# S and dP of a cached attention decode step with K and V as the moving operand, packed into four column tiles of TensorE

## The chip, the cores and the metric

The kernel runs on one NeuronCore of a Trainium2 chip. Its time is the device time of one execution in microseconds (us); three runs before the change gave 403.45, 403.95 and 405.34, so the median is 403.95. Times inside an execution come from one profiled execution. TensorE multiplies matrices into PSUM, VectorE and ScalarE work on SBUF and PSUM, GpSimd and SyncE (SP) mostly issue DMAs here.

## The reference

One decode step of a gated mix of attention over a cache and an MLP, forward and backward. All inputs and outputs are bf16.

```python
def _A_ref(x, k_cache, v_cache, wq, wo):        # H = 32 heads, Sk = 4096, Dh = 128, D = 640
    q = (x @ wq).reshape(B, Sq, H, Dh)...
    scores = einsum("bhqd,bhkd->bhqk", q, k_cache) * (Dh ** -0.5)
    p = softmax(scores)
    o = einsum("bhqk,bhkd->bhqd", p, v_cache)
    return o.reshape(B, Sq, H * Dh) @ wo
def _B_ref(x, w1, b1, w2):                      # F = 1728, Mish
    h = x @ w1 + b1
    return (h * tanh(softplus(h))) @ w2
g = sigmoid((x * gate_w).sum(-1, keepdims=True))
out = g * _A_ref(...) + (1 - g) * _B_ref(...)
# outputs: out and the gradients of x, k_cache, v_cache, wq, wo, w1, b1, w2, gate_w for grad_out
```

With one query row, attention's backward pass needs, per head, dP = dO . V^T (one number per cached position), dS = P * (dP - D) with D = sum(dO * O), dV = P^T dO, dK = dS^T q, and dq = dS K. dK and dV are as large as the caches: 32 x 4096 x 128 each, so the kernel reads 82 MB and writes 82 MB.

## The kernel before, in words

The 32 heads are worked in 16 blocks of two heads (`i`, 0 to 15). In a block's K or V buffer (128 partitions x 8192 bf16, 2 MB) 64 partitions belong to each head and hold 64 positions each. There are seven such buffers; dV and dK are written over V and K and stored from there, and the freed buffer takes the next load. SP issues all loads in a fixed order (`loads`, `pump`); GpSimd issues most stores (`store_kv`).

A block is 16 slots (`slot(i, s)`), written out in order on every engine's queue. The weights `wq` and `wo` (four groups of eight heads) and the MLP are spread over the slots by tables (`plan`, `at`): the sums `do_sum` and `dx_sum` on VectorE, the products `dwo_row`, `dwq_row`, `mlp_dw2` on ScalarE or VectorE.

The scores need K transposed, dP needs V transposed. `transposes(b, c)` takes one eighth of a buffer: four float32 transposes on TensorE (a float32 is a pair of bf16, so a pair of d's stays together) into one of three PSUM tiles `tr`, and one ScalarE copy of 128x512 into a `tch` tile, of which there are NT = 4. In slots 0 to 7 these are V's eighths, in slots 8 to 15 those of the next block's K. `lagged` holds two of them back; then `products` makes eight matmuls from one `tch` tile (four parts t, two bf16 halves e), in which the transposed K or V is the stationary operand and a few columns of q or dO (`qR`, `dR`) move, 48 columns wide. They land in PSUM as `S` or `dP` with positions on the partitions, as the softmax wants them.

The chain of a block, in slots: `soft_max` (2, VectorE, from `S`), `soft_maxt` (4: transpose on TensorE, then negM on VectorE), `soft_exp` (5, ScalarE), `soft_z` (7), `soft_p` (8, ScalarE), `row_sum` for o (7 and 8, TensorE: 16 matmuls in four column tiles with V moving), `take` of o (8: ScalarE copies the PSUM tile into a `tch` tile), `o_post` (9: four transposes and four short VectorE steps), `d_sum` (10: a float32 matmul, then nD on VectorE), `ds_make` (11), the dV quarters `outer` (9, 10, 12, 13, VectorE), dq by `row_sum` (13, 14) and `take`, and the dK quarters (15 and, in the next block, 0, 1, 3). The last block (15) is written out after the loop, with the stores of dV and dK in halves, and then the small outputs from `frow`. Before the loop a prologue makes q, the first S and the first dO.

Of the kernel before, what the change touches and what calls it, by code (L numbers as in the profile page):

```python
# [17 lines left out]
def kernel(  # L18
# [49 lines left out]
    NT = 4  # L68
# [121 lines left out]
    ones_f = C([P, P], F32, "ones_f")  # L190
# [4 lines left out]
    qR = [C([P, 4, 2, 2, 2], BF16, f"qR{t}") for t in range(2)]  # L195
    dR = [C([P, 4, 2, 2, 2], BF16, f"dR{t}") for t in range(2)]
    for t in e_m + rs + ds_m:
        nc.vector.memset(t[:], 0.0)
    for t in qR + dR:
        nc.vector.memset(t[:].rearrange("p a b c d -> p (a b c d)"), 0.0)  # L200
# [12 lines left out]
    sel = C([P, 4, 16, 8], BF16, "sel")  # L213
    idv = idf[:].rearrange("p (a h d) -> p a h d", a=4, h=2)
    nc.vector.tensor_tensor(sel[:], idv[:, :, 0, :].unsqueeze(3).to_broadcast([P, 4, 16, 8]),
                            idv[:, :, 1, :].unsqueeze(3).to_broadcast([P, 4, 16, 8]), ALU.add)
# [46 lines left out]
    def pair_cols(dst):  # L263
# [6 lines left out]
        for jj in range(2):  # L270
            h = slice(64 * jj, 64 * jj + 64)
            nc.scalar.mul(dst[h, :, :, jj, :], tb[h], scale)
# [20 lines left out]
    def do_hot(g):  # L293
        nc.vector.tensor_tensor(R, sel[:], do8[g % 2][:].unsqueeze(1).unsqueeze(1).to_broadcast([P, 4, 16, 8]),
                                ALU.mult)
# [28 lines left out]
    def o_rows(g):  # L324
        ps = misc([P, 16, 8], F32, "o8_ps")
        nc.tensor.matmul(ps[:].rearrange("p a b -> p (a b)"), lhsT=od16[:].rearrange("p a b -> p (a b)"), rhs=idb[:],
                         start=True, stop=True)
        o8m = two.tile([P, 16, 8], F32, name="o8m", tag="o8m", bufs=1)
        nc.vector.tensor_tensor(o8m[:], ps[:], m16[:].unsqueeze(2).to_broadcast([P, 16, 8]), ALU.mult)
        nc.vector.reduce_sum(o8f[:], o8m[:].rearrange("p a b -> p b a"), axis=AX.X)  # L330
        nc.vector.tensor_copy(o8[:], o8f[:])
# [38 lines left out]
    def transposes(b, c):  # L370
        tp = tr_ps.tile([P, 4, P], F32, name="tr", tag="tr")
        src = fview(b)
        for t in range(4):
            nc.tensor.transpose(tp[:, t, :], src[:, 4 * c + t, :], idf[:])  # L374
# [5 lines left out]
    def products(ps, src, c, col):  # L380
        for t in range(4):
            B = 4 * c + t
            for e in range(2):
                nc.tensor.matmul(ps[:, 4 * B:4 * B + W].rearrange("p (a b) -> p a b", b=4),  # L384
                                 lhsT=src[:, t, :, e],
                                 rhs=col[:, e, :, :].rearrange("p a b -> p (a b)").unsqueeze(1).to_broadcast([P, W // 4, 4]),
                                 start=(e == 0), stop=(e == 1))

    S_ps, dP_ps, st = {}, {}, {}
# [5 lines left out]
    def soft_max(i):  # L395
        m = two.tile([P, 1], F32, name="m32", tag="m32")
        for hh in range(2):
            nc.vector.reduce_max(m[HS[hh]], sview(S_ps[i], hh), axis=AX.X)
        st[i] = dict(m=m)
# [9 lines left out]
    def soft_exp(i):  # L409
        for hh in range(2):  # L410
            nc.scalar.activation(e_m[i % 2][HS[hh], 0:J, hh], sview(S_ps[i], hh), ACT.Exp, bias=st[i]["negM"][HS[hh]],  # L411
                                 scale=1.0, accum_out=rs[i % 2][HS[hh], hh:hh + 1])

    def soft_z(i):
        z = chain([P, 2], F32, "z2")
        nc.tensor.matmul(z[:], lhsT=ones_f[:], rhs=rs[i % 2][:], start=True, stop=True)
# [27 lines left out]

    def own_cols(i, key, out):
# [14 lines left out]
    def d_sum(i):  # L460
        d = chain([P, 2], F32, "d2")
        nc.tensor.matmul(d[:], lhsT=ones_f[:], rhs=st[i]["od"][:], start=True, stop=True)
# [4 lines left out]
    def ds_make(i):  # L467
        ds = two.tile([P, J, 2], BF16, name="ds_dup", tag="ds_dup")
        for hh in range(2):
            nc.vector.scalar_tensor_tensor(ds_m[i % 2][HS[hh], 0:J, hh], in0=sview(dP_ps[i], hh),  # L470
# [265 lines left out]
    def lagged(i, s):  # L736
        pend.append((i, s))
        if len(pend) > 2:
            run_products(*pend.popleft())
# [3 lines left out]
    def run_products(i, s):  # L743
        src = work.pop((i, s))
        if s < 8:
            if s == 0:
                dP_ps[i] = one_ps.tile([P, 2 * J + W], F32, name="dP", tag="dP")
            products(dP_ps[i], src, s, dR[(i // 4) % 2][:, i % 4])
        else:
            n = i + 1  # L750
            if s == 8:
                S_ps[n] = one_ps.tile([P, 2 * J + W], F32, name="S", tag="S")
            products(S_ps[n], src, s - 8, qR[(n // 4) % 2][:, n % 4])
# [10 lines left out]
    def slot(i, s):  # L764
# [12 lines left out]
        elif pend:  # L777
            run_products(*pend.popleft())
        if i < 0:
            return  # L780
        if chain_on:
# [6 lines left out]
            if s == 2:  # L788
                soft_max(i)
            if s == 4:  # L790
                soft_maxt(i)
            if s == 7:
                soft_z(i)
        if s == 7:
            row_sum(i, "o", vbuf[i], e_m[i % 2], 0, 8)
        if s == 8:
            row_sum(i, "o", vbuf[i], e_m[i % 2], 8, 16)
            take(i, "o")
        if s == 10:
            d_sum(i)  # L800
# [6 lines left out]
        if s == 9:  # L807
# [24 lines left out]
    nc.tensor.matmul(z_ps[:], lhsT=ones_f[:], rhs=zp[:], start=True, stop=True)  # L832
# [32 lines left out]
    for c in range(8):  # L865
        run_products(-1, 8 + c)
        if c < 4:
            work[(-1, 12 + c)] = transposes(kbuf[0], 4 + c)
    for k in range(8):
# [41 lines left out]
    row_sum(i, "o", vbuf[i], e_m[i % 2], 8, 16)  # L911
    take(i, "o")
    last_dv(0)
    while pend:
        run_products(*pend.popleft())
    o_post(i)
    d_sum(i)
# [38 lines left out]
    nc.tensor.matmul(dg_ps[:], lhsT=ones_f[:], rhs=dgp[:], start=True, stop=True)  # L956
# [11 lines left out]
    frow = C([3, P, RC], BF16, "frow")  # L968
    nc.vector.tensor_copy(frow[:].rearrange("r p c -> r c p"), fr_ps[:])
    flat = frow[:].rearrange("r p c -> r (p c)")  # L970
# [36 lines left out]
```

## Time and profile before

| | |
|---|---|
| median of 3 runs | 403.95 us |
| profiled execution, its own time | 404.45 us |
| span of its instructions | 402.3 us |
| TensorE matmul busy | 303.7 us (76%), 4242 instructions |
| TensorE weight loads busy | 249.0 us (62%), 4249 instructions |
| VectorE busy | 293.4 us (73%) |
| ScalarE busy | 264.2 us (66%) |
| DMA | 164.71 MB, mean 409 GB/s |
| mean granted TensorE clock | 0.915 |
| `products` (L384) on TensorE | 2048 matmuls of 128x48, 94.8 us; their weight loads 89.7 us |
| `transposes` (L374) on TensorE | 1024 of 128x128 float32, 171.6 us |
| copies to `tch` (L377) on ScalarE | 256 of 128x512 at 0.587 us, 145.1 us |
| `take` (L443) on ScalarE | 128x512, 0.585 to 0.592 us each |
| dV and dK quarters (L480) on VectorE | 128 at 1.22 us, 153.6 us |

Busy times are of one execution; TensorE's overlap its weight loads, and the ends of its matmuls are modelled. The page cuts the span into 40 slices of about 10 us and gives the busy share of each in tenths; "DMA" there is the mean of the core's 16 DMA engines. "PEclk" is the clock that the throttle granted TensorE.

### The profile page before, as it was taken

What the parts mean: (1) busy time and instruction counts of PE and PEld (TensorE: products, weight loads), DVE (VectorE), ACT (ScalarE), POOL (GpSimd) and SP (SyncE); (2) the same over time, 40 slices, a digit from 0 to 9 for tenths busy, and PEclk for the clock granted to TensorE, in tenths of its full rate; (3) what the DMA queues carried; (4) which work ended last, traced back from release to release, by engine and by line L of the source; (5) the groups of instructions that cost most, each with busy time, mean ns of one, the idle gap of its engine ahead of it and who ended that gap; (6) DMA issues with size and microseconds to landing.
All of it is one profiled execution on the core that took longest, in us unless ns stands there. A gap on an engine that the chain in (4) does not pass through costs nothing.

```text
span 402.3 us, 10310 instructions
## 1 busy us (share of the span) xinstructions
PE 303.7 (76%) x4242; PEld 249.0 (62%) x4249; DVE 293.4 (73%) x650; ACT 264.2 (66%) x539; POOL 23.6 (6%) x47
## 2 busy tenths in 40 slices
PE   3879977987778675978889969845789898887410
PEld 3567866866567564866678748725568676675200
DVE  3759677789876595979887948751895697788770
ACT  3547453677567867787766668843377998876730
POOL 3000100001000010100001000000000000000000
PEclk9989998999899699999999989988699899999655
DMA  8999999999999999999999999999999999999992
GB/s 274 428 408 428 427 422 423 428 418 389 414 425 426 420 368 427 422 427 429 433 428 423 430 423 435 423 427 427 428 424 433 424 418 425 421 426 428 402 413 83
DMA packets 15867, 164.71 MB, mean 409 GB/s; under 512 B 1624, under 2 KB 1819, under 8 KB 6092
## 3 DMA queue, kind: packets, MB, share of 16 engines
q1 hardware_dynamic: 8842, 94.08, 55.8%
q0 software_dynamic: 5376, 63.42, 37.5%
q10 hardware_dynamic: 1602, 6.56, 4.3%
q8 instruction: 33, 0.54, 0.5%
q14 instruction: 14, 0.11, 0.1%
HBM read 82.03 MB, written 82.03 MB: 408 GB/s over the span
## 4 chain that ended last, share of the span: by engine, by line
DMA 31%; issue 20%; PE 18%; DVE 17%; ACT 9%; POOL 1%; SPq 1%; ACTq 0%; POOLq 0%; DVEq 0%
DMA wq<-in_A_wq_dram 10%; DVE kv L480 9%; PE tr L374 7%; DMA out_dram<-kv 6%; DMA wo<-in_A_wo_dram 6%; DMA wq<-in_B_w_dram 6%; DMA kv<-in_A_k_cache_dram 4%; ACT tch L377 3%; PE tr L448 2%; PE S L384 2%; DVE junk L290 1%; ACT p_dup L424 1%; PE dq L434 1%; PE a_ps L340 1%; ACT tch L443 1%
## 5 line engine op out<-in xcount | busy, mean ns | idle before, releaser
L377 ACT COPY tch<-tr 128x512 f32<-128x512 f32 x256 | 145.1, 587 | 65.3 <-PE tr L374 60.1
L374 PE MATMUL tr<-idf,kv 128*128 128x128 f32 x1024 | 171.6, 294 | 21.1 <-DMA kv<-in_A_v_cache_dram 10.5
L374 PEld LDWEIGHTS tr<-idf,kv 128*128 128x128 f32 x1024 | 119.7, 150 | 49.3 <-issue 32.4
L384 PEld LDWEIGHTS <-tch 128*128 128x128 bf16 x2048 | 89.7, 98 | 21.6 <-ACT tch L377 15.4
L480 DVE TENSOR_TENSOR kv<-p_dup,Dr 128x2048 bf16<-128x2048 bf16 x64 | 76.8, 1220 | 19.7 <-ACT p_dup L424 19.4
L480 DVE TENSOR_TENSOR kv<-ds_dup,Qr 128x2048 bf16<-128x2048 bf16 x64 | 76.8, 1220 | 0.4
L384 PE MATMUL dP<-dR,tch 128*128 128x48 bf16 x1024 | 47.1, 185 | 10.5 <-ACT tch L377 10.3
L384 PE MATMUL S<-qR,tch 128*128 128x48 bf16 x1024 | 47.7, 186 | 1.1 <-ACT tch L377 0.5
L290 DVE SCALAR_TENSOR_TENSOR junk<-wo,da_bc 128x640 bf16<-128x640 bf16 x32 | 26.3, 822 | 13.8 <-DMA wo<-in_A_wo_dram 13.1
L448 PE MATMUL tr<-idf,tch 128*128 128x128 f32 x128 | 22.0, 297 | 18.2 <-ACT tch L443 18.0
L757 POOL DMA_DIRECT2D out_dram<-kv x25 | 13.4, 536 | 297.1 <-DVE kv L480 251.9
L448 PEld LDWEIGHTS tr<-idf,tch 128*128 128x128 f32 x128 | 14.0, 145 | 20.8 <-ACT tch L443 19.8
L352 ACT ACTIVATE wq<-dqrow,xf 128x1024 bf16<-128x1024 bf16 (+2 forms) x30 | 25.1, 860 | 2.6 <-DVE wq L507 2.3
L507 DVE SCALAR_TENSOR_TENSOR wq<-wq,dqrow 128x1024 bf16<-128x1024 bf16 (+2 forms) x30 | 25.1, 863 | 0.2
L434 PE MATMUL o<-kv,e_m 128*32 128x512 bf16 x256 | 20.4, 400 | 0.0
L434 PE MATMUL dq<-kv,ds_m 128*32 128x512 bf16 x256 | 19.5, 384 | 0.9 <-DVE ds_m L470 0.9
L424 ACT ACTIVATE p_dup<-e_m,rz 64x128 bf16<-64x128 bf16 x32 | 12.7, 397 | 7.7 <-DVE rz L418 7.3
L352 ACT ACTIVATE wo<-da_bc,o8f 128x640 bf16<-128x640 bf16 x20 | 15.9, 825 | 1.3 <-PE a_ps L340 0.8
L411 ACT ACTIVATE e_m<-S,negM 64x64 bf16<-64x64 f32 x32 | 10.5, 329 | 6.3 <-DVE negM L406 5.7
L281 ACT CAST Qr<-q_ps 64x256 bf16<-64x256 f32 x16 | 5.9, 367 | 12.3 <-PE q_ps L277 12.2
L474 ACT COPY ds_dup<-ds_m 64x128 bf16<-64x128 bf16 x32 | 9.5, 296 | 6.4 <-DVE ds_m L470 5.8
L602 DVE SCALAR_TENSOR_TENSOR junk<-wq,db_bc 128x640 bf16<-128x640 bf16 (+1 forms) x14 | 11.5, 820 | 1.9 <-ACT db_bc L256 1.7
(169 smaller groups left out, 279.2 us busy)
## 6 DMA issues: line engine op xcount, KB each, us to landing
out_dram<-kv POOLq DMA_DIRECT2D x25, 2048.0 KB, 16.7
kv<-in_A_v_cache_dram SPq DMA_DIRECT2D x16, 2048.0 KB, 24.0
kv<-in_A_k_cache_dram SPq DMA_DIRECT2D x15, 2048.0 KB, 20.3
out_dram<-kv SPq DMA_DIRECT2D x5, 2048.0 KB, 29.3
wo<-in_A_wo_dram SPq DMA_DIRECT2D x4, 1280.0 KB, 42.9
out_dram<-kv SPq DMA_DIRECT2D x4, 1024.0 KB, 15.5
out_dram<-wo POOLq DMA_DIRECT2D x3, 1280.0 KB, 23.5
wq<-in_A_wq_dram SPq DMA_DIRECT2D x2, 1280.0 KB
```

Of the source, the lines that this page charges most:

```text
L290: nc.vector.scalar_tensor_tensor(junk[:], in0=wob[g % 2][:, k, :], scalar=1.0, in1=da_bc[:], op0=ALU.mult, op1=ALU.mult, accum_out=do8[g % ...
L352: nc.scalar.mul(dst, src, col)
L374: nc.tensor.transpose(tp[:, t, :], src[:, 4 * c + t, :], idf[:])
L377: nc.scalar.copy(dst[:].rearrange("p a b e -> p (a b e)").bitcast(F32), tp[:].rearrange("p a b -> p (a b)"))
L384: nc.tensor.matmul(ps[:, 4 * B:4 * B + W].rearrange("p (a b) -> p a b", b=4), lhsT=src[:, t, :, e], rhs=col[:, e, :, :].rearrange("p a b - ...
L424: nc.scalar.activation(p[HS[hh]], e_m[i % 2][HS[hh], 0:J, hh].unsqueeze(2).to_broadcast([64, J, 2]), ACT.Copy, scale=st[i]["rz"][HS[hh], h ...
L434: nc.tensor.matmul(st[i][key][c:c + 32].rearrange("p a b -> p (a b)"), lhsT=cols[:, 4 * g:4 * g + 16, :].rearrange("p a b -> p (a b)"), rh ...
L448: nc.tensor.transpose(tp[:, 126 * t:126 * t + P], st[i][key + "r"][:, t, :], idf[:])
L480: nc.vector.tensor_tensor(kview(b)[:, j0:j0 + n, :].rearrange("p j (a b) -> p j a b", b=2), col[:, j0:j0 + n, :].unsqueeze(2).to_broadcast ...
L507: nc.vector.scalar_tensor_tensor(w, in0=w, scalar=1.0, in1=dqrow[g % 2][:, c0:c1], op0=ALU.mult, op1=ALU.mult, accum_out=dq_acc[:, rc, par ...
L602: nc.vector.scalar_tensor_tensor(junk[0:n, :], in0=w2row(k), scalar=1.0, in1=db_bc[0:n, :], op0=ALU.mult, op1=ALU.mult, accum_out=dact[0:n ...
L757: eng.dma_start(dst, bufs[b][:, 0:J * Dh])
```

## The change

Now q or dO is the stationary operand (32 columns) and the transposed K or V moves, 512 columns at a time. Two eighths (chunks) and the two bf16 halves of each make four such matmuls with outputs in the four 32-partition column tiles (`run_batch`); four batches accumulate into one PSUM tile `Sr` or `dPr`, where `qR`/`dR` is a band of zeros with the wanted columns in the middle, so that each batch writes its own rows. The tile then has positions along the free dimension. ScalarE copies it to a `tch` tile (`take`), and `back` turns it to positions on partitions and adds the halves in one step: four float32 matmuls with the copy as stationary operand and a 0/1 matrix `sel2` (32 columns) moving. The order of parts in `transposes` is changed to fit.

The wait before a batch is longer (LAG 3, two at a time), there are five `tch` tiles, and some steps move: `soft_max` from slot 2 to 3 (now behind the dK quarter of slot 3), `row_sum` of o from 7 and 8 to 6 and 7, its `take` from 8 to 7 (now ahead of `soft_p`), `o_post` from 9 to 8. `back` of S stands in slot 2, `back` of dP in slot 10 ahead of `d_sum`. Some constants and temporaries are made smaller or share memory (`ones_f`, `sel`, `o8m`, `frow`).

```diff
-    NT = 4
+    NT = 5
+    LAG = 3
-    qR = [C([P, 4, 2, 2, 2], BF16, f"qR{t}") for t in range(2)]
+    qR = [C([P, 10, 16], BF16, f"qR{t}") for t in range(2)]
...
+    sel2 = C([P, 2, 2, 8], F32, "sel2")
...
         for t in range(4):
-            nc.tensor.transpose(tp[:, t, :], src[:, 4 * c + t, :], idf[:])
+            B = 16 * (c // 4) + 4 * t + 2 * (c % 2) + c // 2 % 2
+            nc.tensor.transpose(tp[:, t, :], src[:, B, :], idf[:])
...
-    def products(ps, src, c, col):
-        for t in range(4):
-            B = 4 * c + t
-            for e in range(2):
-                nc.tensor.matmul(ps[:, 4 * B:4 * B + W].rearrange("p (a b) -> p a b", b=4),
-                                 lhsT=src[:, t, :, e],
-                                 rhs=col[:, e, :, :].rearrange("p a b -> p (a b)").unsqueeze(1).to_broadcast([P, W // 4, 4]),
-                                 start=(e == 0), stop=(e == 1))
...
+    def back(i, key):
+        ps = one_ps.tile([P, 2 * J], F32, name=key, tag=key)
+        v = ps[:].rearrange("p (u t x) -> p t u x", u=2, t=4)
+        for t in range(4):
+            nc.tensor.matmul(v[:, t], lhsT=st[i][key + "r"][:, t, :], rhs=sel2[:].rearrange("p u k x -> p u (k x)"),
+                             start=True, stop=True)
+        st[i][key] = ps
...
     def lagged(i, s):
         pend.append((i, s))
-        if len(pend) > 2:
-            run_products(*pend.popleft())
+        if len(pend) > LAG:
+            run_batch()
...
+    def run_batch():
+        part = [pend.popleft() for _ in range(2)]
+        i, s = part[0]
+        key, n, col = ("dP", i, dR) if s < 8 else ("S", i + 1, qR)
+        u, q = s % 8 // 2, n % 4
+        if u == 0:
+            st[n][key] = one_ps.tile([P, 4, P], F32, name=key + "r", tag=key)
+        out = st[n][key][:].rearrange("p a b -> p (a b)")
+        cf = col[n // 4 % 2][:].rearrange("p a b -> p (a b)")
+        for k, x in enumerate(part):
+            src = work.pop(x)[:].rearrange("p a b e -> p (a b) e")
+            for e in range(2):
+                r, c0 = 64 * k + 32 * e, 16 * (2 * q + e) + 12 - 4 * u
+                nc.tensor.matmul(out[r:r + 32], lhsT=cf[:, c0:c0 + 32], rhs=src[:, :, e],
+                                 start=(u == 0), stop=(u == 3), tile_position=(0, r))
+        if u == 3:
+            take(n, key)
...
             if s == 2:
+                back(i, "S")
+            if s == 3:
                 soft_max(i)
...
+        if s == 6:
+            row_sum(i, "o", vbuf[i], e_m[i % 2], 0, 8)
         if s == 7:
-            row_sum(i, "o", vbuf[i], e_m[i % 2], 0, 8)
-        if s == 8:
             row_sum(i, "o", vbuf[i], e_m[i % 2], 8, 16)
             take(i, "o")
+        if s == 10:
+            back(i, "dP")
         if s == 10:
             d_sum(i)
...
-        if s == 9:
+        if s == 8:
             o_post(i)
...
     soft_p(i)
-    row_sum(i, "o", vbuf[i], e_m[i % 2], 8, 16)
-    take(i, "o")
+    run_batch()
     last_dv(0)
-    while pend:
-        run_products(*pend.popleft())
     o_post(i)
+    back(i, "dP")
     d_sum(i)
     ds_make(i)
```

## The prediction

> **What bounds the kernel now.** I read the page's slices first.
>
> ```profile
> PEclk9989998999899699999999989988699899999655
> DMA  8999999999999999999999999999999999999992
> GB/s 274 428 408 428 427 422 423 428 418 389 414 425 426 420 368 427 422 427 429 433 428 423 430 423 435 423 427 427 428 424 433 424 418 425 421 426 428 402 413 83
> ```
>
> From the second slice to the last but one the sixteen DMA engines are 90% busy or more and move about 427 GB/s. No engine row of the page stays at 9 like that. So the first question for any change of compute is what it does to the transfers. Next, stretches of 5 us (TensorE, its weight loads, VectorE, ScalarE, GpSimd, granted clock, DMA share, GB/s).
>
> ```profile
> 90.00:95.00 5.00, 4.57 (x69) 3.95 (x68) 4.30 (x9) 4.91 (x11) 0.53 (x1) 1.00 0.95 347
> 270.00:275.00 5.00, 2.40 (x21) 2.31 (x22) 0.00 (x0) 0.86 (x2) 0.00 (x0) 0.50 1.01 428
> 330.00:335.00 5.00, 3.25 (x46) 2.23 (x46) 3.15 (x6) 4.92 (x8) 0.00 (x0) 1.00 1.01 414
> 395.00:400.00 5.00, 0.00 (x0) 0.00 (x0) 0.00 (x0) 0.00 (x0) 0.00 (x0) 0.50 0.06 26
> ```
>
> Only at 90 does the share sag before the end: the V store of block 2 is issued at 90.26, and there compute was what the transfers waited for. At 270 the order is reversed: compute idles. At 330 ScalarE is full. The last row is 26 GB/s, one sixteenth of 427: for some 6 us a single late DMA engine finishes alone (finer slices show 22 to 44 GB/s until 400.4, and the span ends at 402.3). The waits say where compute waited for loads:
>
> ```profile
> DVE junk L290 <- DMA wo<-in_A_wo_dram: 13.1, 1, 13.1
> PE tr L374 <- DMA kv<-in_A_v_cache_dram: 10.5, 4, 6.9
> PE tr L374 <- DMA kv<-in_A_k_cache_dram: 10.3, 4, 6.4
> ```
>
> The wait for wo ends at 280.40. From there to the last store compute runs without waiting for a load, in blocks of 18.5 to 20 us. The chain shows how a block closes on itself (start, length, engine, tile, line):
>
> ```profile
> 343.16 2.26 DVE kv L480 x2
> 345.41 0.13 DVE m L398
> 345.56 0.23 DVE m L398
> 345.81 1.23 DVE kv L480
> 347.07 0.23 DVE negM L406
> ...
> 350.46 0.62 ACT wq L352
> 351.08 0.30 ACT p_dup L424
> ...
> 352.30 0.60 ACT tch L443
> 352.94 0.65 PE tr L448 x4
> ...
> 354.27 0.38 PE d L462 x2
> ```
>
> dK quarters, maximum, exponential, a ScalarE stretch to p, then o, D, and dV quarters again. TensorE is a small part of it. Prices come from the timeline:
>
> ```profile
> 349.02 0.36 PE L416 MATMUL z<-rs,ones_f 128*128 128x2 f32 x2
> 349.31 0.62 PE L434 MATMUL o<-kv,e_m 128*32 128x512 bf16 x8
> 350.25 0.36 PEld L384 LDWEIGHTS <-tch 128*128 128x128 bf16 x8
> 391.58 4.88 SPq L976 DMA_DIRECT2D out_dram<-frow  x5
> ```
>
> **Removed from and added to TensorE.** A block has 16 steps, each with eight weight loads and products (0.36 us): 5.8 us go. In their place come eight batches of four 32-column products of 512 moving columns. The row sums are of that form: eight took from 349.31 to 349.86, so four cost 0.28, eight batches 2.2 us; if the two-element step of the moving operand halved the rate, 4.4. Turning back is four float32 products, and z shows that one such product is two passes (0.29 to the next load, 349.02 to 349.31): 1.2 us each, twice per block, 2.4; the transposes' 0.11 per pass would make it 0.9 each. TensorE gets 5.8 - 2.2 - 2.4 = 1.2 us per block back (bounds: 1.0 dearer, 1.8 cheaper). I take it as nothing at the end: in the TensorE stretch of the chain from 304.9 to 310.2 five steps save about 0.2 each, and the one new turning back in it costs 1.2. If TensorE were the bound there, the bounds are those of its sum.
>
> **Added to ScalarE.** Two copies of 128x512 per block at 0.59 (row of L443): 1.2 us, 19 us in all, 264 to 283. Where they stand in the queue matters, not their sum. LAG 3 and the fifth tch buffer cost nothing as long as TensorE's steps run ahead of ScalarE; without that cover each batch would wait for one copy, 0.59.
>
> **Moved on the chain, from block 12 on, where nothing waits for loads.**
> (a) The copy of o now precedes p on ScalarE. In blocks 12 to 15 ScalarE is what p waits for (350.46 to 351.08), and the first dV quarter queues behind p on VectorE: 4 x 0.59 = 2.4 us. Where p waits for rz behind VectorE's sums (block 2, block 11), nothing.
> (b) The maximum goes behind the third dK quarter. Its length was on the chain before; what is new is its transpose on TensorE, which the quarter used to hide: 0.30 plus a semaphore, 0.4 us a block, 1.6 in four.
> (c) D's sum is queued on TensorE behind the turning back of dP, which waits for the new copy on ScalarE, which is queued behind two tch copies and, in blocks 13 and 14, a weight product (L352). From the end of p to nD it was 2.9 us (351.79 to 354.69). Now: 0.58 + 0.58 + 0.59 + 1.2 + 0.4 = 3.4, plus 1.15 in block 13 and 0.72 in block 14. VectorE's second dV quarter and ds wait for nD. o itself is earlier and no longer counts. So +0.5 in blocks 11 and 12, +1.6 and +1.2 in 13 and 14, 0 in 15 (its order there differs): 3.8 in all.
> Sum (a) to (c): 7.8 us at the last stores and at frow. Below, 3: (c) hidden but for the weight products, and (a) for half. Above, 12: with half clock on top.
>
> **The cover at the end.** frow's five copies are issued from 391.58 to 396.46, 2.7 us of it waiting for kv transfers (a row of SP's waits); the lone DMA engine works until 400.4. frow may come 400.4 - 396.9 = 3.5 us later without moving the end, and up to 2.7 more if its own wait goes as the queue empties: 3.5 to 6.2; I take 5. The last dK half has more room, since the late engine still holds older work. Of 7.8 us, 2.8 remain.
>
> **The front and the fetches.** Block 2's V store (90.26) carries (c) with two q casts (0.75) in the queue, +1.2, less about 0.7 from the TensorE stretch at 66 to 74: +0.5, at full price since the transfers already sag. Blocks 3 and 4 can add up to 2: I keep that for the range. Before 65.9 TensorE waited 2.5 us for a load, so the head's changes are covered; from 150 to 285 the 20 us of load waits cover 1 to 2 us a block. Instructions: 4096 of TensorE's 8491 go, 1024 and 512 come, 30% fewer. The page gives their fetch (queue 8: 33 packets, 0.54 MB) 0.5% of sixteen engines' span, 2.0 us; 30% is -0.6. The Trainium skill, "Runtime: NRT & Kernel Launch", "Instruction fetch mechanics", calls crossing a 16 KiB block mostly hidden; by that this term is 0 and the sum 0.6 higher, while here the packets do take DMA time.
>
> **Sum.** 404.45 is the profiled execution (span 402.3 and 2.15 around it). 404.45 + 2.8 + 0.5 - 0.6 = 407.15. That execution lay 0.5 above the median of 403.95, so 406.6, 0.7% slower. About 0.5% (2.0 us) is what a measurement of this kernel can tell from no change.
>
> **Rivals.**
> Hidden by the transfers: the delay stays within the cover, because (c) is short or the weight products fall elsewhere. For it: the DMA rows. Against: ScalarE at 4.92 of 5. Time: 403.95 - 0.6 = 403.4, no change.
> Faster: both copies fall into ScalarE's 34% of idle time, turning back costs 0.45, stores leave earlier, and the late DMA engine, whose stretch at one sixteenth lasts some 6 us, ends half as late: -3 - 0.6 + 0.4 gives 400.8. For it: p to nD would be 2.6. Against: nothing shows that this engine's lag comes from compute.
> Clock: the stretch at 270 follows idle time and runs at 0.50, where four transposes took 0.92 (317.68 in the chain) against 0.48. TensorE now waits for ScalarE at each turning back; four more such stretches of 3.4 us on the chain, three steps of 0.44 each, add 5.3: 411.9. It decides once TensorE is busy under half of a stretch. The Trainium skill, "TensorE: Matmul & The Clock Gate", "What's actually happening", says the same: half rate is the default, and an idle window of about 3.4 us returns to it; the trace agrees (0.50 at 270). Against: by the sums above TensorE's work falls only 19 of 304 us. That the four column tiles don't run at once (0.39 per product, mean of L434's rows, so +10 us of TensorE per block) would end there too; the row sums speak against it.
>
> **How the numbers follow.** Forecast (tail beyond its cover, 404.6 to 410) 0.50, of which 0.40 lies more than 0.5% up; hidden 0.30; faster 0.12; clock 0.08. So faster 0.12, same 0.40, slower 0.48. The range reaches down past the hidden case to its lower side, 402.0, and up to the sum with 12 in place of 7.8, rounded up, 411.0; the faster case and most of the clock are left out. The forecast's own range is 404.6 to 410.
>
> **What would show it.** Right: p to nD at 3.4 us or more in blocks 12 to 14; the copy of o ahead of p; negM about 0.4 behind m; frow issued near 399; the 26 GB/s stretch gone or overtaken; DMA at 9 until then. TensorE's busy time near 285, ScalarE's near 283. Wrong: turning back at 0.5 us, frow still issued before 395, or a DMA row with new gaps between 100 and 280.

## The result and the profile after

The changed kernel takes 420.78 us (median of 6 runs, 416.96 to 422.60) against 404.48 us (6 runs, 403.45 to 405.54): a ratio of 1.040, 95% interval 1.035 to 1.045. The forecast was 406.6 with a range of 402 to 411: the side was right, the size was not. The profiled execution is the fastest of the six (416.96, span 415.2), so the profile explains 12.9 us of span (415.2 - 402.3) and not all of the 16.3 between the medians. The other five executions had a lower granted clock (0.903 to 0.911 against 0.918), and the two slowest, 422.28 and 422.60, had 0.903 and 0.907. In the tables below, executions of a slower state of the chip (one or two in each of e2, e4, e11 and e14) are left out.

First the page of the kernel after: the busy line, the DMA and GB/s rows of the 40 slices, and the shares of the chain that ended last.

```profile
PE 337.6 (81%) x2965; PEld 222.6 (54%) x2969; DVE 291.6 (70%) x652; ACT 278.5 (67%) x571; POOL 23.7 (6%) x47
DMA  8999999999999999999999999999999999999457
GB/s 277 421 398 429 427 414 429 428 367 356 423 425 389 401 396 352 396 370 437 428 426 422 426 426 432 397 424 433 429 429 431 425 426 427 427 414 400 199 216 278
PE 47%; ACT 19%; DMA 15%; DVE 10%; issue 6%; SPq 1%; ACTq 0%; DVEq 0%
```

ScalarE's 278.5 is near the 283 of the forecast. TensorE's 337.6 is not near 285: it was 303.7 before, and it rose although 30% fewer instructions run on it. The chain says what follows from that: before, the DMA engines had 31% of it and TensorE 18%; now TensorE has 47% and the DMA engines 15%. The two windows answer to those at 90 and 395 us of before (TensorE, weight loads, VectorE, ScalarE, GpSimd, granted clock, DMA share, GB/s):

```profile
90.00:95.00 5.00, 4.83 (x49) 2.73 (x48) 4.87 (x10) 4.85 (x11) 0.53 (x1) 1.00 0.74 265
395.00:400.00 5.00, 1.16 (x29) 1.02 (x26) 3.81 (x5) 3.64 (x5) 0.00 (x0) 0.50 0.13 52
```

The sag at 90 is deeper (265 GB/s, 347 before), and at 395, where one late DMA engine used to finish alone, the transfers now stand nearly idle (a share of 0.13) while compute still works towards the last stores. The waits of after:

```profile
DVE nD L469 <- PE d L467: 24.3, 15, 3.0
PEld dP L446 <- ACT tch L440: 22.6, 16, 2.9
PE dP L446 <- ACT tch L440: 18.6, 16, 2.6
PE tr L380 <- DMA kv<-in_A_k_cache_dram: 6.1, 1, 6.1
```

The last line is all that is left of the waits for K, V and wo, and it falls in the first 40 us. Before, these waits were 13.1 us for wo and 20.8 us for K and V (7.3 of them in the first 40 us). From there on compute is so far behind the transfers that it no longer waits for K, V or wo. The first three lines are the turning back of dP (L446): TensorE stands there for ScalarE's copy (L440) once a block, and VectorE stands for D's sum (L467), which is queued behind it. One such place, from the chain of after (start, length, engine, tile, line), and below it three rows of the timeline that follow it:

```profile
344.20 1.15 ACT wq L357
345.34 0.47 ACT tch L383
345.82 0.50 ACT tch L440
...
346.36 1.08 PE dP L446 x8
347.44 0.33 PE d L467 x2
```

```profile
347.63 1.09 PE L380 MATMUL tr<-idf,kv 128*128 128x128 f32 x4
347.81 0.16 DVE L469 COPY nD<-d 128x2 f32<-128x2 f32 x1 [2.99 <-PE d L467]
348.82 0.59 ACT L383 COPY tch<-tr 128x512 f32<-128x512 f32 x1 [2.02 <-PE tr L380]
```

The copy of dP's sums is third in ScalarE's queue, behind a weight product and a copy of transposes. TensorE idles 2.48 us until it is through. The next transposes stand behind the turning back in TensorE's queue, so ScalarE, once it has caught up, has nothing to copy and idles 2.02 us in its turn; VectorE idles 2.99 us for nD. These transposes also take 1.09 us where the same four took 0.60 at 342.35 (shown further down): the granted clock is 0.50 from 347.5 to 350.5 and was 1.00 from 342 to 346. Three engines lose over 2 us each at one place, one after the other.

Where the 12.9 us come from is read off the starts of p, block by block:

| start of p, us | block 3 | block 4 | block 10 | block 11 | block 15 | span |
|---|---|---|---|---|---|---|
| before | 104.0 | 132.8 | 256.7 | 291.6 | 368.3 | 402.3 |
| after | 107.4 | 142.7 | 274.4 | 298.6 | 385.8 | 415.2 |
| later by | 3.4 | 9.9 | 17.7 | 7.0 | 17.5 | 12.9 |

Up to block 10 the kernel loses 17.7 us beyond what the waits for K and V take up. The wait for wo, which stood ahead of block 11, takes up 10.7 of them. The other 7.0 come through, the four steps from p of block 11 to p of block 15 (the late blocks, from here on) add 10.5, and the cover at the end takes 4.6 back.

### The profile page after: what moved, and what is told of

Its sections match the earlier page's. It is cut to its first block, busy times and chain, and to the rows that moved or that the text cites. A ratio compares the mean times of both kernels' runs of the same rounds, so it can differ in the third digit from the quotient of the medians.

```text
span 415.2 us, 7814 instructions
## 1 busy us (share of the span) xinstructions
PE 337.6 (81%) x2965; PEld 222.6 (54%) x2969; DVE 291.6 (70%) x652; ACT 278.5 (67%) x571; POOL 23.7 (6%) x47
## 4 chain that ended last, share of the span: by engine, by line
PE 47%; ACT 19%; DMA 15%; DVE 10%; issue 6%; SPq 1%; ACTq 0%; DVEq 0%
PE tr L380 17%; DMA wq<-in_A_wq_dram 9%; ACT tch L383 7%; DMA wq<-in_B_w_dram 6%; ACT tch L440 5%; DVE kv L485 5%; PE Sr L761 3%; PE S L446 3%; PE dP L446 3%; PE dq L431 3%; PE tr L453 3%; PE dPr L761 3%; PE o L431 2%; ACT wq L357 2%; PE a_ps L345 2%
## 5 line engine op out<-in xcount | busy, mean ns | idle before, releaser
L380 PEld LDWEIGHTS tr<-idf,kv 128*128 128x128 f32 x1024 | 122.4, 152 | 52.3 <-issue 25.6
L485 DVE TENSOR_TENSOR kv<-p_dup,Dr 128x2048 bf16<-128x2048 bf16 x64 | 76.7, 1220 | 5.4 <-ACT p_dup L421 4.8
L446 PE MATMUL dP<-sel,tch 128*128 128x32 f32 x128 | 17.4, 280 | 18.6 <-ACT tch L440 18.6
L761 PE MATMUL Sr<-tch,qR 128*32 128x512 bf16 x256 | 29.3, 436 | 0.7 <-ACT qR L277 0.5
L446 PEld LDWEIGHTS dP<-sel,tch 128*128 128x128 f32 x128 | 15.6, 192 | 22.6 <-ACT tch L440 22.6
L761 PE MATMUL dPr<-tch,dR 128*32 128x512 bf16 x256 | 26.6, 405 | 0.0
L446 PE MATMUL S<-sel,tch 128*128 128x32 f32 x128 | 17.7, 284 | 7.5 <-ACT tch L440 7.5
L431 PE MATMUL dq<-kv,ds_m 128*32 128x512 bf16 x256 | 22.0, 423 | 0.9 <-DVE ds_m L475 0.9
L446 PEld LDWEIGHTS S<-sel,tch 128*128 128x128 f32 x128 | 16.3, 200 | 10.7 <-ACT tch L440 10.6
L403 DVE TENSOR_REDUCE negM<-mt 64x1 f32<-64x64 f32 x32 | 7.1, 223 | 19.0 <-PE mt L400 18.4
L469 DVE COPY nD<-d 128x2 f32<-128x2 f32 x16 | 2.5, 159 | 24.3 <-PE d L467 24.3
```

The costliest lines, as they stand in the source:

```text
L380: nc.tensor.transpose(tp[:, t, :], src[:, B, :], idf[:])
L431: nc.tensor.matmul(st[i][key][c:c + 32].rearrange("p a b -> p (a b)"), lhsT=cols[:, 4 * g:4 * g + 16, :].rearrange("p a b -> p (a b)"), rh ...
L446: nc.tensor.matmul(v[:, t], lhsT=st[i][key + "r"][:, t, :], rhs=sel2[:].rearrange("p u k x -> p u (k x)"), start=True, stop=True)
L485: nc.vector.tensor_tensor(kview(b)[:, j0:j0 + n, :].rearrange("p j (a b) -> p j a b", b=2), col[:, j0:j0 + n, :].unsqueeze(2).to_broadcast ...
L761: nc.tensor.matmul(out[r:r + 32], lhsT=cf[:, c0:c0 + 32], rhs=src[:, :, e], start=(u == 0), stop=(u == 3), tile_position=(0, r))
```

## The experiments

Four theories of the loss were set against each other. Q: TensorE waits in its own queue for ScalarE's copies, and what stands behind it waits too. S: ScalarE's two added copies a block cost their time. T: TensorE's own added time costs. M: the moved steps cost. The kernels are variants of after, or of before where the table says so.

| run | median us | ratio to before, 95% interval |
|---|---|---|
| e1_moves (on before) | 405.02 | 0.999 (0.996 to 1.001) |
| e2_takes_vector | 417.51 | 1.033 (1.027 to 1.039) |
| e3_back_late | 405.81 | 1.002 (0.999 to 1.004) |
| e4_back_double | 459.31 | 1.131 (1.122 to 1.140) |
| e6_dsum_first | 413.40 | 1.021 (1.017 to 1.025) |
| e9_s_late | 411.42 | 1.016 (1.009 to 1.023) |
| e10_dp_late | 410.47 | 1.012 (1.009 to 1.015) |
| e8_back_quarter | 408.03 | 1.007 (1.004 to 1.009) |
| e11_late_double | 420.78 | 1.039 (1.033 to 1.044) |
| e13_late_quarter | 403.05 | 0.995 (0.993 to 0.998) |
| e14_contiguous | 419.49 | 1.035 (1.028 to 1.041) |
| e5_lag2 | 429.10 | 1.059 (1.053 to 1.064) |
| e15_products_twice (on before) | 409.85 | 1.014 (1.010 to 1.017) |
| e16_products_half (on before) | 407.70 | 1.008 (1.005 to 1.010) |
| e17_late_transposes | 411.91 | 1.020 (1.014 to 1.025) |
| e18_wait_only (on before) | 414.16 | 1.022 (1.015 to 1.028) |
| e19_wait_late (on before) | 409.09 | 1.010 (1.007 to 1.014) |

The kernel before ran at 404.5 to 405.6 us beside them.

**e1_moves: the moved steps alone, in the kernel before.**

```
-            if s == 2:
+            if s == 3:
                 soft_max(i)
...
+        if s == 6:
+            row_sum(i, "o", vbuf[i], e_m[i % 2], 0, 8)
         if s == 7:
-            row_sum(i, "o", vbuf[i], e_m[i % 2], 0, 8)
-        if s == 8:
             row_sum(i, "o", vbuf[i], e_m[i % 2], 8, 16)
             take(i, "o")
...
-        if s == 9:
+        if s == 8:
             o_post(i)
...
```

> The kernel before with three of the steps moved as the change moves them and nothing else: the sum over the row of o one slot earlier (slots 6 and 7, its copy ahead of p), o's own columns at slot 8, the maximum at slot 3 behind the third quarter of dK. No column tiles for S and dP, no added copies, no turning back. Theory M (the moved steps are the cost: 2.4 us and 1.6 us over the late blocks in the prediction's sum): 407 to 412 us. Theories Q (TensorE waits in its own queue for ScalarE's copies), S (ScalarE's two added copies a block) and T (TensorE's own added time): none of them is in this kernel, so 403 to 406 us, no change from before.

405.02 us: no change. M falls. The moves even help the late blocks: from the end of p to nD it is 1.3 us in blocks 12 to 14 against 2.9 before, and from p of block 11 to p of block 15 it is 74.6 us against 76.7. The end doesn't move with it: p of block 15 starts at 368.5 us against 368.3, since p of block 11 is 2.3 later.

**e2_takes_vector: the two copies by VectorE.**

```
+        if key in ("S", "dP"):
+            nc.vector.tensor_copy(st[i][key + "r"], st[i][key][:])
+        else:
             nc.scalar.copy(st[i][key + "r"], st[i][key][:])
```

> The kernel after, with the copies of the four-tile sums of S and dP (128x512, two a block) made by VectorE in place of ScalarE. Theory S (ScalarE's time, 2 x 0.59 us a block, 19 us in all): the time goes back to 405 to 410 us. Theory Q (turning back stands in TensorE's queue until the copy has come through the copying engine's queue): the copy now stands behind up to two quarters of 1.22 us on VectorE in place of ScalarE's copies and scalings, and VectorE gets 19 us more of work at 70% busy: 412 to 420 us. Theory T (TensorE's own added time): 419 to 423 us. Theory M (moved steps): 419 to 423 us.

417.51 us, within Q's bounds, but not a clean test of S: block 0's p starts at 37.5 us instead of 30.8. At the front VectorE now stands 5.3 us at the copy until TensorE has made the first S, and sums that ran before that now come behind it. The four late blocks take 84.2 us against 87.2. Something is gained per block and lost at the start.

**e3_back_late: turning back one slot later.**

```
-            if s == 2:
-                back(i, "S")
             if s == 3:
+                back(i, "S")
                 soft_max(i)
...
         if s == 10:
-            back(i, "dP")
-        if s == 10:
             d_sum(i)
         if s == 11:
+            back(i, "dP")
             ds_make(i)
```

> The kernel after, with both turnings back one slot later on TensorE (S at slot 3 behind the first batch of dP, dP at slot 11 behind D's sum), so that a slot more of transposes lies between the copy and the products that need it, and D's sum is no longer queued behind them. Nothing else moves: the maximum stays at slot 3, ds at slot 11. Theory Q: the waits of TensorE for these copies (33 us over the run at this line in the trace of after) shrink to a third and the time falls to 408 to 414 us. Theories S and T: no work is taken away, 419 to 423 us. Theory M: D's sum is ahead again, 418 to 420 us.

405.81 us: 15 of the 16 us are gone, more than Q's own figure, with every copy, batch and product still there. This run decides against S and T as causes by themselves. TensorE's idle time ahead of the turning back falls from 59.3 us to the first line below, and the waits again hold the load of wo that had vanished. (These sums take the rows of the weight loads and of the products together, so most of the time stands in them twice; for the products alone it falls from 26.1 us to 1.5.)

```profile
  ACT tch L440: 7.5, 15
DVE junk L295 <- DMA wo<-in_A_wo_dram: 10.1, 1, 10.1
```

Compute is again ahead of the transfers when wo is due, near 280 us.

**e4_back_double: the products made twice.**

```
-        for t in range(4):
+        for t in (0, 1, 2, 3, 0, 1, 2, 3):
```

> The kernel after, with the float32 products that turn S and dP back made twice over (1.08 us more of TensorE twice a block, 34 us in all); the copies and all waits stay. Theory T (TensorE's time is the bound from block to block): nearly all of it shows, 440 to 455 us. Theory Q (the chain waits on ScalarE at this place, then TensorE catches up): the added 1.08 us lie in the chain of each block as well but are partly covered by the transfers that wait, 428 to 440 us. Theory S (ScalarE is the bound): under half shows, 421 to 430 us.

459.31 us, above all three ranges: 38.5 us more for 34 us of work by the length of the rows (29 by the distance between starts). That it all comes from the products isn't shown: the granted clock of the profiled execution fell too, to 0.879 against 0.918.

**e6_dsum_first: D's sum ahead of the turning back of dP.**

```
         if s == 10:
-            back(i, "dP")
-        if s == 10:
             d_sum(i)
+            back(i, "dP")
```

> The kernel after with D's sum issued ahead of the turning back of dP at slot 10; the turning back stays at slot 10 and still stands in TensorE's queue until ScalarE's copy is through. The prediction's term (c) put the delay of D's sum at 3.8 us over the late blocks. If the delay of D's sum was what the later turning back cured: 410 to 416 us. If it is the wait of TensorE itself, with the next transposes behind it (theory Q): 419 to 422 us, and TensorE's idle time ahead of these products stays near 59 us (both rows of the line).

413.40 us, in the range of the first of the two readings: 7 us are gained. But the trace doesn't put them down to the wait for nD. In the late blocks that wait shrinks (from the end of p to nD 6.2 us in all, 13.8 in after) and the stretch is as long as before the edit, 87.4 us against 87.2: ds now waits for dP, and the next maximum comes later. The gain lies ahead of block 11, whose p starts 5.3 us earlier. TensorE's idle time at the turning back stays at 50.3 us.

**e9_s_late and e10_dp_late: one of the two turnings back later.**

```
e9_s_late:    back(i, "S")  at slot 3 in place of 2, nothing else
e10_dp_late:  back(i, "dP") at slot 11 in place of 10, nothing else
```

> The kernel after with only the turning back of S one slot later (slot 3 in place of 2). Its waits were 7.5 us (products) and 10.6 us (weight loads) of the trace of after, against 18.6 and 22.6 for dP, so theory Q shares the 15 us that both together gave in the ratio of the waits: 3 to 6 us from S, 415 to 418 us. If S's way to the maximum is what counts in the chain of blocks (ds to the next maximum grew most from before to after): 408 to 413 us.

> The kernel after with only the turning back of dP one slot later (slot 11 in place of 10, behind D's sum). By theory Q and the ratio of the waits: 9 to 12 us of the 15, 408 to 412 us. If S's way to the maximum is what counts: 416 to 420 us.

411.42 and 410.47 us, so 9 us from S and 10 us from dP, where both together bring 15. S's 9 is uncertain: its four executions fall into two pairs, 408.5 and 409.2 us at a granted clock of 0.92, 413.6 and 414.5 at 0.90. The ratio of the waits foretold S wrongly. That the two gains don't add up fits a second one that reaches the transfers, which isn't shown apart.

**e8_back_quarter: cheap products, the wait kept.** (It leaves out three quarters of the sums.)

```
-        for t in range(4):
-            nc.tensor.matmul(v[:, t], lhsT=st[i][key + "r"][:, t, :], rhs=sel2..., ...)
+        nc.tensor.matmul(v, lhsT=st[i][key + "r"][:, 0, :], rhs=sel2...to_broadcast([P, 4, 2, 16]), ...)
```

> The kernel after with each turning back made as one float32 product of 128 columns on the first quarter of the copied sums in place of four of 32 columns: three quarters of the sums are left out, so S and dP hold other values. TensorE's work at this line falls from 1.08 us to some 0.4 us twice a block, about 20 us in all; the wait for the copy stays where it was. Theory T (the added products' own time; doubling them gave +40 us for 34 us of products): 398 to 408 us. Theory Q (the wait, not the products): the wait stays and only the products' part on the chain goes, 410 to 417 us. Both may hold, as the doubled run suggests: 406 to 412 us.

408.03 us, at the edge of T's range and in that of both: 13 us come back though TensorE still waits 57.9 us for the copies. So the wait without the products costs little here, as the products without the wait do in e3_back_late. Both lie, one behind the other, on the way from the copy to the maximum and to ds, with all of the next transposes behind them. Shorten either and the blocks nearly keep up with the transfers.

**e11_late_double: e3_back_late with the loop of e4_back_double.**

> The kernel with both turnings back one slot later (405.8 us), and their float32 products made twice over as in the doubled run. From start to the next group's start one turning back holds TensorE 0.91 us in the trace of after, so the doubling adds 1.8 us a block, 29 us in all. Theory Q alone (the wait was the whole cost, and TensorE has room once it is gone): 405 to 412 us. Theory T beside Q (TensorE's occupancy sets the pace of the blocks; the wait for wo, 10.1 us in the run with late turning back, and the loads take up the first part of it): 11 blocks by 1.8 less 10 is 10, and 5 blocks by 1.8 is 9, so 420 to 428 us.

420.78 us, as T beside Q said. With the wait gone there is no room for 1.8 us more per block on that way: of the 29 us added, 15 show.

**e13_late_quarter: e3_back_late with the product of e8_back_quarter.**

> Both reliefs at once: turning back one slot later (alone 405.8 us), and only one float32 product of 128 columns for each on the first quarter of the sums (three quarters left out, S and dP hold other values; alone 408.0 us). If compute still set the end, the second relief would bring 5 to 10 us more: 396 to 401 us. If the transfers set it once the blocks keep up (theory F: all 16 DMA engines are busy in before's trace and the wait for wo stands at 280 us): 402 to 405 us, no faster than before, with the wait for wo back at 13 us or more.

403.05 us against 405.04: half a percent, with three quarters of the sums left out. The wait for wo is back at 16.0 us. Compute waits for the transfers again, and this second saving on TensorE brought 3 us on e3_back_late's 405.81 and not the 5 to 10 that it would have if compute still set the end.

**e14_contiguous: the batch without the step of two.**

```
-            src = work.pop(x)[:].rearrange("p a b e -> p (a b) e")
+            src = work.pop(x)[:].rearrange("p a b e -> p (a b e)")
...
-                ... rhs=src[:, :, e],
+                ... rhs=src[:, 512 * e:512 * e + 512],
```

> The kernel after with the batches' moving operand read as 512 neighbouring bf16 elements in place of every second one (the same tiles, the same count of elements; the values that meet in a product are others, so S and dP differ). It asks whether the step of two in the moving read costs TensorE time: a batch holds TensorE 0.34 us from its start to the next group's start, and takes 0.41 us by its rows, against 0.31 us a round for the same shape in the sums over the row, which read neighbours. If the step is the cause: 0.24 to 0.30 us a batch, 5 to 13 us less over 128 batches, 408 to 416 us. If the weights and the four tiles are: 419 to 422 us.

419.49 us, and a batch holds TensorE 0.33 us against 0.34: the step costs nothing.

**e5_lag2: batches one chunk earlier.**

```
-    LAG = 3
+    LAG = 2
```

> The kernel after with batches issued one chunk earlier (lag of 2 in place of 3): the last batch of dP falls to slot 8 and that of S to slot 0, so the copy stands a slot further ahead of its turning back, which stays at slots 10 and 2. Theory Q: the wait at the turning back goes as it does with the later turning back, but each batch now stands one slot behind its own copies and TensorE may wait there: 407 to 414 us if that costs under 0.5 us a block, 415 to 425 us if it costs more. Theory T alone: 419 to 422 us.

429.10 us, worse than any range. The wait at the turning back is nearly gone (3.6 us), but the batches now wait 36.4 us (20.2 for S, 16.2 for dP) for the copies of their own chunks, and VectorE still waits for D's sum (30.8 us). The wait has moved forward.

**e15_products_twice and e16_products_half: TensorE's time alone, in the kernel before.**

```
-        for t in range(4):
+        for t in [t for _ in range(2) for t in range(4)]:          # e15
+        for t in [t for _ in range(2 - c % 2) for t in range(4)]:  # e16
```

> The kernel before with the eight small products of every chunk of S and dP made twice over into the same columns (same result), and nothing else: TensorE's time is added with no new copy, no new wait and no moved step. From start to the next group's start such a group holds TensorE 0.20 us in the trace of before (its rows last 0.36 us, since they overlap the next), so it adds 16 x 0.20 = 3.2 us a block. Theory T (TensorE's occupancy alone lengthens the blocks, and what the waits for loads and for wo can't take up shows): 11 blocks by 3.2 less some 25 us of such waits is 10, 4 late blocks by 3.2 less 4.5 us of cover is 8, so 418 to 426 us. By the rows' 0.36 us it would be 5.8 us a block: 440 us or more. Theory Q alone (only TensorE's wait for a copy costs): 404 to 408 us.

> As the run above, but only every second chunk's products are made twice: 1.6 us a block more of TensorE, nearly what the two turnings back hold (1.8 us), again without any wait for a copy. Theory T: the first 11 blocks' 18 us vanish in the waits for loads, the late four add 6.4 us less 4.5 us of cover, 404 to 409 us; it would be the twin of the run with late turning back (405.8 us). If occupancy of 1.6 to 1.8 us a block were the whole loss of the change, without the waits: 414 to 420 us.

409.85 and 407.70 us: for the first, T's 418 to 426 and Q's 404 to 408 are both missed; T's 404 to 409 for the second holds. The windows from p of block 11 to p of block 15 show why (columns as above; in order: before, after, e3_back_late, e15_products_twice):

```profile
291.60:368.30 76.70, 66.67 (x1003) 55.70 (x1004) 61.77 (x130) 64.39 (x130) 3.81 (x6) 0.98 1.01 424
298.60:385.80 87.20, 74.07 (x688) 48.90 (x686) 61.53 (x130) 67.65 (x139) 3.83 (x6) 0.98 1.00 422
292.90:373.90 81.00, 73.75 (x688) 48.02 (x686) 61.06 (x128) 67.50 (x139) 3.82 (x6) 1.00 1.01 426
294.80:373.40 78.60, 75.56 (x1505) 66.56 (x1504) 61.95 (x130) 64.22 (x130) 3.82 (x6) 1.00 1.01 421
```

Length less TensorE's busy time is its idle time: 10.0 us before, 3.0 in e15_products_twice. Work spread over the steps in small groups fills the idle time: 8.9 us more work make the stretch only 1.9 longer. (Its granted clock was higher as well, 0.948 over the execution against 0.915, which hides part of the added work.) After has 7.4 us more work and yet 13.1 us of idle time, and 8.8 of these stand ahead of the two turnings back (dP 5.4, S 3.4), with the work queued behind. In e3_back_late, with nearly the same work as after, the idle time is 7.2 and hardly any of it stands there.

**e17_late_transposes: a cheaper turning back, whole result.**

```
-            nc.tensor.matmul(v[:, t], lhsT=st[i][key + "r"][:, t, :], rhs=sel2..., start=True, stop=True)
+            nc.tensor.transpose(tp[:, t, :], st[i][key + "r"][:, t, :], idf[:])
...
+        for u in range(2):
+            nc.vector.reduce_sum(ps[:, 64 * u:64 * u + 64]..., tp...[:, :, :, :, u, :], axis=AX.X)
```

> The kernel with late turning back, where the float32 products are replaced by four transposes (0.49 us from start to the next group's start, against 0.91 us) and two sums by VectorE (128x64 by 2 terms each): a version that computes the whole result. Theory T with the floor of the transfers: TensorE gets 0.8 us a block back, VectorE has two sums of some 0.2 us more in the chain, so 402 to 405 us, no faster than before beyond what can be told. If VectorE's queue makes the sums wait behind quarters of 1.22 us: 406 to 411 us.

411.91 us. VectorE gets 19 us of sums. At the front it stands 6.7 us for TensorE's transposes of the first S, and block 0's p starts at 39.8 us instead of 29.7 in e3_back_late; the late stretch is no shorter (82.7 against 81.0). No version tried that computes the whole result is faster than before.

**e18_wait_only and e19_wait_late: the waits alone, in the kernel before.**

```
+    def copy_again(i, key):     # ScalarE, 128x512: dq at slot 1, o at slot 9
+        dst = tch[tcount[0] % NT]
+        ...
+        nc.scalar.copy(st[i]["again"], st[i][key][:])
+    def need(i):                # slots 2 and 10 (e18), 3 and 11 (e19)
+        mt = chain([P, P], F32, "mt")
+        nc.tensor.transpose(mt[:], st[i]["again"][:, 0, :], idf[:])
```

> The kernel before with the waits of the change and almost none of its TensorE time: ScalarE copies a 128x512 sum once more (o's at slot 9, dq's at slot 1), and one single transpose on TensorE needs that copy at slots 10 and 2, where the change turns back; its output is not used. ScalarE gets 2 x 0.59 us a block, TensorE 2 x 0.15 us. Theory Q (TensorE standing in its queue for the copy, the next transposes behind it, so that the idle time can no longer be filled): 409 to 416 us. Theory of occupancy alone, or ScalarE's copies costing nothing (as the run with the copies on VectorE said): 404 to 406 us.

> The control of the run above: the same copies and the same two transposes in the kernel before, but needed one slot later (11 and 3). Theory Q: the wait is gone, 404 to 407 us, clearly under the run above. If the difference between the two runs is under 1.5 us, the two copies themselves are the cost (theory S), or nothing is.

414.16 us, and 409.09 with the need a slot later. TensorE's idle time ahead of these 30 transposes, first in e18_wait_only, then in e19_wait_late:

```profile
  ACT tch L449: 16.4, 26
```

```profile
  ACT tch L449: 0.4, 2
```

With hardly any products, the waits cost 5 us (executions of 411.3 to 416.5 us with them, 408.0 to 410.4 without). The two copies, the ring of four buffers that they share, and the two transposes cost 4 us without the waits, more than Q said; part of that may be the clock, which was 0.92 in the late stretch of both runs against 0.98 before. With the 3 us of e16_products_half that is 12 of after's 16. These are three different kernels, and that their costs add is not shown; nor does any run take the other 4 us apart.

## Why the prediction was wrong, step by step

**TensorE's balance: mis-sized, and in sign.** The forecast took 0.36 us for a group of eight products, the length of its row, and had TensorE 1.2 us per block ahead. Rows of TensorE overlap. What a group costs its queue is the distance from its start to the next group's start. Two stretches that wait for nothing, of before and of after:

```profile
327.90 0.63 PE L374 MATMUL tr<-idf,kv 128*128 128x128 f32 x4
328.38 0.36 PE L384 MATMUL dP<-dR,tch 128*128 128x48 bf16 x8
328.58 0.64 PE L374 MATMUL tr<-idf,kv 128*128 128x128 f32 x4
```

```profile
342.35 0.60 PE L380 MATMUL tr<-idf,kv 128*128 128x128 f32 x4
342.88 0.41 PE L761 MATMUL dPr<-tch,dR 128*32 128x512 bf16 x4
343.22 0.66 PE L380 MATMUL tr<-idf,kv 128*128 128x128 f32 x4
```

Before, a chunk is 0.48 for the transposes and 0.20 for the products: two chunks are 1.36 us. After, two chunks are 0.49 from one set of transposes to the next instruction of that kind, 0.53 to the batch and 0.34 for the batch: 1.36 us again. The removed work was 3.2 us a block and not 5.8, and the batches give all of it back. The two turnings back, 0.91 us each from start to next start (forecast 1.2), come on top: 1.8 us a block, and the windows above say the same (74.07 - 66.67 over four blocks is 1.85). The forecast was 3 us a block off. This alone doesn't make the loss: e3_back_late has the same work and loses next to nothing. What does is the time that TensorE stands ahead of each turning back, which the forecast priced only as far as D's sum waits behind it, in (c).

**"From 150 to 285 the 20 us of load waits cover 1 to 2 us a block": failed, and cost most.** The blocks lost more than that: 14.3 us over the seven from p of block 3 to p of block 10, and 2.6 us each in the late ones. The first eleven use up the waits for K and V, then the wait for wo, and 7.0 us come through. "Blocks 3 and 4 can add up to 2", kept for the range, was 6.5 between their p alone. Block 2's V store, forecast 0.5 us later, is 3.1 later (90.26 to 93.39). The sign that was named against the forecast, new gaps between 100 and 280, shows in the GB/s row (slices of 352 to 401); the digits of the DMA row stay at 9.

**(a) and (b), 4.0 us: there, but paid back.** In e1_moves, over the late blocks, the time from negM to p grows by 3.0 us and that from the end of ds to negM by 0.9, against the 2.4 and 1.6 of the forecast. But from the end of p to nD it shrinks by 6.0, so the moves alone gain 2.1. The forecast saw that the copy of o goes ahead of p ("o itself is earlier and no longer counts") and gave the earlier o no credit.

**(c), 3.8 us: right in kind, half its size.** From the end of p to nD it was to be 3.4 us in blocks 11 and 12, 4.55 and 4.1 in 13 and 14; it is 3.0, 3.0, 4.2 and 3.7. Against before that is only 1.8 us more over the four (before had 3.35 in block 11, where the forecast took 2.9). But the right base is the kernel with the moves alone, where it is 6.1 us in all against 13.8: the turning back ahead of D's sum costs 7.8 us there. Of the 12.5 us by which after's late blocks are longer than those of e1_moves, 2.8 more lie between the maximum and negM, which came 1.05 to 1.36 us behind m and not the forecast 0.4 (0.42 in e1_moves, 0.41 to 0.75 in e3_back_late). No term held this. The time from ds to the next maximum, longer than before (9.5 us on average against 8.1), is nearly the same in e1_moves (9.3) and so isn't the loss either. As e6_dsum_first shows, moving D's sum alone is not enough: then ds waits for dP instead. e3_back_late, with e18_wait_only and e19_wait_late, shows the cause: TensorE standing at the turning back with all of its queue behind it.

**The cover at the end, 5 us: right.** 17.5 us at block 15's p became 12.9 at the span's end: 4.6.

**ScalarE, fetches, rivals.** ScalarE's added copies have the 19 us of the forecast by their rows (its busy time grew 14.3), and their place in the queue did matter more than their sum. The fetches fell from 33 packets to 23 as forecast, but with the transfers no longer the bound that could buy nothing. Column tiles that don't run at once fall: four products of 512 columns last 0.41 us together.

The clock rival doesn't fall. The mean granted clock of the whole execution hides it (0.918 against 0.915), since before had much of its half clock between p of block 10 and p of block 11, where compute waited for wo (0.80 there, 0.93 in after). Between p of block 3 and p of block 10, where after lost 14.3 us, the difference stands out (first from p of block 3 to p of block 4, then to p of block 10; before, after, before, after, and last e3_back_late to block 10):

```profile
104.00:132.80 28.80, 20.61 (x308) 17.05 (x306) 20.17 (x38) 20.04 (x39) 1.10 (x2) 0.97 1.01 422
107.40:142.70 35.30, 27.91 (x224) 18.15 (x223) 20.68 (x42) 21.26 (x41) 1.10 (x2) 0.81 0.98 405
104.00:256.70 152.70, 123.34 (x1775) 102.42 (x1776) 120.22 (x231) 112.08 (x224) 9.07 (x17) 0.95 1.01 422
107.40:274.40 167.00, 144.04 (x1225) 93.58 (x1225) 119.50 (x230) 118.51 (x238) 9.10 (x17) 0.91 0.99 409
106.00:259.40 153.40, 136.58 (x1226) 90.19 (x1225) 119.76 (x230) 117.45 (x237) 9.09 (x17) 0.96 1.01 424
```

The traces here have only the two values 1.00 and 0.50, so a mean of 0.91 over 167 us is some 30 us at 0.50, against some 15 before. If all TensorE's work there lay on the chain, the 15 us more would cost half of that, 7 to 8 of the 14.3 us (an estimate from these rows, and an upper bound). In the late blocks the clock is 0.98 in both, and after loses 10.5 us all the same, so the waits cost without it too. That the waits brought the half clock fits the place at 346 us above, where it follows TensorE's 2.48 us of idle time, and e3_back_late, where both shrink together; no run holds the one and changes the other.

## What to carry to other kernels

Cost TensorE's work by the distance between starts in a stretch that waits for nothing; the lengths of overlapping rows overstate what a removal gives. When an instruction needs a result that another engine has only just been asked for, price everything that stands behind it in its own queue, and look first whether one slot of other work fits between the two: here that slot was worth 15 us, some of it perhaps through the clock. Read the granted clock in the stretch that lost time; the mean of the execution can hide it. Waits that are to cover a loss are a purse spent once: multiply the loss per block by all blocks ahead of the wait before calling it hidden.

## What was not expected of the hardware

Reading the batches' moving operand with a step of two bf16 elements costs TensorE no more than reading neighbours: 0.33 against 0.34 us for four products of 512 columns in four column tiles. And eight weight loads with eight products of 48 columns hold TensorE for only 0.20 us, so that four column tiles at 0.34 for two chunks, with the 0.05 more of the transposes ahead of them, save nothing over two such groups.
